# An attention and Hyena kernel: one list scheduler orders all engines, and keys, queries and x are turned by DMA

## The chip, the cores and the metric

The kernel runs on one NeuronCore of a Trainium2 chip. The core's engines are TensorE (PE), VectorE (DVE), ScalarE (ACT), GpSimd (POOL) and SyncE (SP, which here only issues DMAs). Sixteen DMA engines carry the transfers of all queues. The metric is the device time of one execution in microseconds (us), less is better.

## The reference

There are 8 batches, 12 heads, 448 positions and 64 dimensions a head (768 in all). First attention with a softmax whose denominator has one more term, then a gated convolution over the 448 positions, done by a Fourier transform:

```python
def _attn_ref(q, k, v):
    scores = scale * np.matmul(q, k.transpose(0, 1, 3, 2))
    m = np.max(scores, axis=-1, keepdims=True)
    e = np.exp(scores - m)
    attn = e / (np.sum(e, axis=-1, keepdims=True) + np.exp(-m) + 1e-09)
    return np.matmul(attn, v).astype(np.float32)

def _moe_ref(x, w_proj, filter_fft, w_out):
    proj = x @ w_proj
    x1, x2, x3 = (proj[..., :D].copy(), proj[..., D:2 * D].copy(), proj[..., 2 * D:].copy())
    X2 = np.fft.rfft(x2, n=S, axis=1)
    H = np.fft.rfft(filter_fft, n=S, axis=0)[None, :, :]
    x2_conv = np.fft.irfft(X2 * H, n=S, axis=1)
    y = x1 * x2_conv * x3
    return (y @ w_out).astype(np.float32)
```

Inputs and outputs are float32; x is the output of attention with the heads side by side.

## The kernel before

Work goes by batch, and in attention by pair of heads (six pairs a batch). For a pair, `transposes` (L321) turns keys and queries on PE with a matmul against the identity (L327, L329); DVE copies them out of PSUM, the keys into `kz`, where each head's keys stand beside zeros (L337, L338), the queries into `qT` (L345; L341 for batch 0, whose rows come in another order). `scores` (L348) has four steps: step 0 with the rest rows of both heads (L357, ACT's exponential at L359), steps 1 to 3 with two matmuls of 448 columns and an exponential of 896 (L353, L355). `attn_out` (L362) multiplies with the values in two halves (L367, L372); DVE divides by the sum (L380 to L382) into `xb`. `back` (L389) turns `xb` on PE (L395) and DVE copies it into `xT` (L398). After three pairs `folds` (L400) adds and subtracts halves of `xT` into `xf`.

`dense` (L463) makes a list of items for a batch: gate projections G (L508), the projection P of the folded x (L473, evicted by ACT at L480 into x2), the spectrum Z (L492 to L501), the inverse transform V (L532 to L547) and the output projection (L558, L580): four row tiles of 112 positions with two column halves, eight groups of six matmuls a batch. ACT evicts them (L568, L587) and SP stores them. "Dense stage" below is the run of these items for one batch. It runs beside the attention of the next batch, so that a period holds one attention and one dense stage; that of the last batch runs alone.

The order on PE, DVE, ACT and POOL is the order in which the program emits the calls (`manual_schedule`, L620). The main loop emits the attention items in a fixed order and after each takes dense items off the list in proportion to the cost, `RATIO = 1.9` (L615, L664). SP is ordered by the framework.

Batch 0 is loaded by SP in long rows as float32 into a stage of three buffers (`staged_load`, L130; casts on DVE and POOL, L160 to L182; the shared rest rows of keys by L164). Batches 1 to 7 are loaded by POOL's queue, which casts to bf16 on the way (`attn_load`, L111: four DMAs for queries at L115, eight for keys at L122 and L123, one for values at L124, then two copies of the rest rows of values, L109). The weights and the filter also come over POOL's queue (L282, L311, L317). `tables` (L185) builds the tables of the Fourier transform on DVE and ACT before anything else on DVE, and `filter_spectrum` (L292) transforms the filter with 16 matmuls (L303, L306) behind batch 0's attention.

Of the kernel before, what the change touches and what calls it, by code (L numbers as in the profile page):

```python
# [18 lines left out]
D = H * DH  # L19
# [8 lines left out]
Q0 = [0, 128, 256, 320]  # L28

# [6 lines left out]
BLK_K = [FQ, FQ, SP, SP]  # L36


@with_exitstack
def kernel(  # L40
# [13 lines left out]
    MAGIC = 12582912.0  # L54

# [7 lines left out]
    qtp = ctx.enter_context(tc.tile_pool(name="qtp", bufs=2))  # L63
# [21 lines left out]
    kn = [const.tile([128, NHP, 4, 128], BF16, name=f"kn{i}") for i in range(2)]  # L85
    vn = [const.tile([128, NHP, 7, DH + 1], BF16, name=f"vn{i}") for i in range(2)]
    vr = [const.tile([128, NHP, 2, DH + 1], BF16, name=f"vr{i}") for i in range(2)]
    kz = [const.tile([128, 8, 128], BF16, name=f"kz{i}") for i in range(3)]

    def constants(i):  # L90
        nc.gpsimd.memset(kn[i][:, :, 0, :], 0.0)
        nc.gpsimd.memset(vr[i], 0.0)
        nc.gpsimd.memset(vn[i][:, :, :, DH : DH + 1], 1.0)
        for u in range(2):
            nc.gpsimd.memset(vr[i][64 * u : 64 * u + 64, :, u, DH : DH + 1], 1.0)


    def batch_tiles(b):
        A = {"b": b, "kn": kn[b % 2], "vn": vn[b % 2], "vr": vr[b % 2]}
        A["qf"] = ld.tile([SP, NST, H, DH], BF16, name="qf")  # L100
        A["xb"] = xbp.tile([128, NST, H, DH], BF16, name="xb")
        A["xT"] = xtp.tile([128, NDT, S + 2], BF16, name="xT")
        A["xf"] = fold.tile([128, 4, NDT, FQ + 1], BF16, name="xf", tag="xf")
        return A

    def rest(A):
        for u in range(2):
            c = slice(64 * u, 64 * u + 64)
            nc.gpsimd.tensor_copy(A["vr"][c, :, u, 0:DH], A["vn"][c, :, 3, 0:DH])  # L109

    def attn_load(b):  # L111
        A = batch_tiles(b)
        kr = k[b].rearrange("h s d -> (h s) d").rearrange("(g t p) d -> p g t d", t=7, p=128)
        for st in range(NST):
            nc.gpsimd.dma_start(  # L115
                A["qf"][:, st, :, :],
                q[b, :, st * SP : (st + 1) * SP, :].rearrange("h p d -> p h d"),
            )
        for u in range(2):
            c = slice(64 * u, 64 * u + 64)  # L120
            for t in range(3):
                nc.gpsimd.dma_start(A["kn"][:, :, 1 + t, c], kr[:, :, 4 * u + t, :])  # L122
            nc.gpsimd.dma_start(A["kn"][c, :, 0, c], kr[c, :, 3, :])  # L123
        nc.gpsimd.dma_start(  # L124
            A["vn"][:].rearrange("p g t d -> p (g t) d")[:, :, 0:DH],
            v[b].rearrange("h s d -> (h s) d").rearrange("(n p) d -> p n d", p=128),
        )
        return A

    def staged_load(b, sp, tp):  # L130


        A = batch_tiles(b)
        A["staged"] = True

        def rows(x, hp):
            o = x[b, 2 * hp].offset
            return bass.AP(x.tensor, o, [[3 * DH, 128], [512 * DH, 2], [1, 3 * DH]])

        def shared(x):  # L140
            o = x[b].offset + 384 * DH
            return bass.AP(x.tensor, o, [[DH, 128], [2 * S * DH, NHP], [1, DH]])

        for hp in range(NHP):
            for name, x in (("k", k), ("q", q), ("v", v)):
                if name == "q":
                    t = A["sq", hp] = sp.tile([SP, 2, NST, DH], F32, name="sq")
                    nc.sync.dma_start(
                        t[:].rearrange("p u j d -> p u (j d)"),
                        q[b, 2 * hp : 2 * hp + 2].rearrange("u (p j) d -> p u (j d)", j=NST),  # L150
                    )
                    continue
                t = A[f"s{name}", hp] = sp.tile([128, 2, 3, DH], F32, name=f"s{name}")
                nc.sync.dma_start(t[:].rearrange("p u j d -> p u (j d)"), rows(x, hp))
                if hp == 0:
                    R = A[f"s{name}r"] = tp.tile([128, NHP, DH], F32, name=f"s{name}r")
                    nc.sync.dma_start(R, shared(x))
        return A

    def cast_shared(A, name, eng):  # L160
        for u in range(2):
            c = slice(64 * u, 64 * u + 64)
            if name == "k":
                eng.tensor_copy(A["kn"][c, :, 0, c], A["skr"][c])  # L164
            else:
                eng.tensor_copy(A["vr"][c, :, u, 0:DH], A["svr"][c])

    def cast_k(A, hp, eng):
        eng.tensor_copy(
            A["kn"][:, hp, 1:4, :].rearrange("p j (u d) -> p u j d", u=2), A["sk", hp]  # L170
        )

    def cast_q(A, hp, eng):
        dst = A["qf"][:, :, 2 * hp : 2 * hp + 2, :].rearrange("p j u d -> p u j d")
        if eng is nc.scalar:
            eng.copy(dst, A["sq", hp])
        else:
            eng.tensor_copy(dst, A["sq", hp])

    def cast_v(A, hp, eng):  # L180
        for u in range(2):
            eng.tensor_copy(A["vn"][:, hp, 4 * u : 4 * u + 3, 0:DH], A["sv", hp][:, u])  # L182


    def tables(tp):  # L185
        ci = tp.tile([128, HALF], I32, name="ci")
        nc.gpsimd.iota(ci[:], pattern=[[1, HALF]], base=0, channel_multiplier=0)
        pi = tp.tile([128, 1], I32, name="pi")
        nc.gpsimd.iota(pi[:], pattern=[[0, 1]], base=0, channel_multiplier=1)
        col = tp.tile([128, HALF], F32, name="col")  # L190
        nc.vector.tensor_copy(col, ci)
        row = tp.tile([128, 1], F32, name="row")
        nc.vector.tensor_copy(row, pi)
        col2 = tp.tile([128, 2, FQ], F32, name="col2")
        row2 = tp.tile([128, 2], F32, name="row2")
        for odd in range(2):
            nc.vector.tensor_scalar(
                col2[:, odd, :], col[:, 0:FQ], 2.0, float(odd), op0=ALU.mult, op1=ALU.add
            )
            nc.vector.tensor_scalar(  # L200
                row2[:, odd : odd + 1], row, 2.0, float(odd), op0=ALU.mult, op1=ALU.add
            )
# [8 lines left out]
        back = tp.tile([128, 1], F32, name="back")  # L211
        nc.vector.tensor_scalar(back, row, -1.0, float(SP), op0=ALU.mult, op1=ALU.add)
        inv = tp.tile([128, 1], F32, name="inv")
        nc.vector.tensor_scalar(inv, half, 2.0 / S, None, op0=ALU.mult)

        NF = 4 * FQ
        NB = 4 * HALF

        def sines(ph, n, tag):
            rd = hyp.tile([128, 2 * NF], F32, name="rd", tag="x2")  # L220
            nc.vector.tensor_scalar(rd[:, :n], ph, 1.0 / S, MAGIC, op0=ALU.mult, op1=ALU.add)
            nc.vector.tensor_scalar(rd[:, :n], rd[:, :n], -MAGIC, None, op0=ALU.add)
            nc.vector.scalar_tensor_tensor(
                ph, rd[:, :n], -float(S), ph, op0=ALU.mult, op1=ALU.add
            )
            sn = hyp.tile([128, 2 * NF], F32, name="sn", tag=tag)
            nc.scalar.activation(sn[:, :n], ph, AF.Sin, scale=float(2.0 * np.pi / S) * SHRINK)
            return sn

        pf = fold.tile([128, 2 * NF], F32, name="pf", tag="xf")  # L230
        pb = hyp.tile([128, NB], F32, name="pb", tag="yT")
        for pg in range(4):
            odd = int(BLK_ODD[pg])
            off = float(SP) if BLK_COS[pg] else 0.0
            nc.vector.tensor_scalar(
                pf[:, pg * FQ : (pg + 1) * FQ],
                col2[:, odd, :],
                row[:, 0:1],
                off,
                op0=ALU.mult,  # L240
                op1=ALU.add,
            )
            nc.vector.tensor_scalar(
                pf[:, NF + pg * FQ : NF + (pg + 1) * FQ],
                col2[:, odd, :],
                back[:, 0:1],
                off + (float(HALF) if pg in (1, 2) else 0.0),
                op0=ALU.mult,
                op1=ALU.add,
            )  # L250
            nc.vector.tensor_scalar(
                pb[:, pg * HALF : (pg + 1) * HALF],
                col,
                row2[:, odd : odd + 1],
                off,
                op0=ALU.mult,
                op1=ALU.add,
            )
        sf = sines(pf, 2 * NF, "yh")
        nc.vector.tensor_scalar(  # L260
            ft[:].rearrange("p a b -> p (a b)"), sf[:FQ, 0:NF], half[:FQ, 0:1], None, op0=ALU.mult
        )
        nc.vector.tensor_scalar(
            fr[:].rearrange("p a b -> p (a b)"),
            sf[:FQ, NF : 2 * NF],
            half[:FQ, 0:1],
            None,
            op0=ALU.mult,
        )
        sb = sines(pb, NB, "g")  # L270
        nc.vector.tensor_scalar(
# [148 lines left out]
    def attention():  # L420
# [4 lines left out]
        for p in range(len(pairs) + 1):  # L425
# [32 lines left out]
            for part in range(3):  # L458
                fd(part)
# [241 lines left out]
```

## Time and profile before

| | us |
|---|---|
| median of 3 runs | 472.2 (471.85 to 473.31) |
| the profiled execution | 474.68 |
| its span, first to last instruction | 472.9 |
| granted TensorE clock, mean | 0.988 |

The profile is of one execution. Its page gives busy time by engine, strips of 40 equal slices of the span with the busy share in tenths, and the costliest groups of instructions. In a row of groups stand: line, engine, operation, output tile, arrow, input tiles, shapes and count; behind the first bar busy us and mean ns of one; behind the second the idle us of the engine just before them and what ended it. In rows by order of time the first two numbers are start and duration. A matmul's duration contains its way through the array, which overlaps the next one, so its cost in a stream is the distance between starts.

### The profile page before, as it was taken

What the parts mean: (1) busy time and instruction counts of PE and PEld (TensorE: products, weight loads), DVE (VectorE), ACT (ScalarE), POOL (GpSimd) and SP (SyncE); (2) the same over time, 40 slices, a digit from 0 to 9 for tenths busy, and PEclk for the clock granted to TensorE, in tenths of its full rate; (3) what the DMA queues carried; (4) which work ended last, traced back from release to release, by engine and by line L of the source; (5) the groups of instructions that cost most, each with busy time, mean ns of one, the idle gap of its engine ahead of it and who ended that gap; (6) DMA issues with size and microseconds to landing.
All of it is one profiled execution on the core that took longest, in us unless ns stands there. A gap on an engine that the chain in (4) does not pass through costs nothing.

```text
span 472.9 us, 9624 instructions
## 1 busy us (share of the span) xinstructions
PE 426.3 (90%) x3872; PEld 298.9 (63%) x3872; DVE 307.3 (65%) x892; ACT 288.2 (61%) x493; POOL 109.4 (23%) x146
## 2 busy tenths in 40 slices
PE   0276889999999999999999999999999999999995
PEld 0144457577766777577766777577766777567664
DVE  7778555785569665774579575874578565873450
ACT  1364557666675667566675657657676668563543
POOL 5816391061202610071103510081000000000000
PEclk9998889999999999999999999999999999999999
DMA  7999999099901993097902991096900110003003
GB/s 208 181 231 176 146 161 62 1 73 134 89 1 11 138 129 19 1 88 120 89 1 20 144 129 5 1 101 126 69 1 1 60 60 0 2 2 119 0 1 116
DMA packets 128492, 35.62 MB, mean 75 GB/s; under 512 B 116925, under 2 KB 124864, under 8 KB 128448
## 3 DMA queue, kind: packets, MB, share of 16 engines
q0 software_dynamic: 118080, 19.87, 55.8%
q1 hardware_dynamic: 10368, 15.14, 10.9%
q8 instruction: 30, 0.49, 0.4%
q14 instruction: 14, 0.11, 0.1%
HBM read 43.86 MB, written 11.01 MB: 116 GB/s over the span
## 4 chain that ended last, share of the span: by engine, by line
PE 67%; DVE 14%; ACT 7%; DMA 7%; POOL 3%; issue 1%; SPq 1%; ACTq 0%; DVEq 0%; POOLq 0%
PE pps L508 18%; PE pps L473 10%; PE ops L580 10%; PE sc L353 9%; PE op L372 5%; DMA wproj_bf<-in_moe_w_proj_dram 4%; PE ops L558 3%; ACT xs L493 3%; PE cps L532 2%; PE xsp L492 2%; DVE t L496 2%; PE xps L395 2%; DVE g L519 2%; PE op L367 2%; DVE t L497 2%; ACT e L355 2%
## 5 line engine op out<-in xcount | busy, mean ns | idle before, releaser
L355 ACT ACTIVATE e<-sc 128x896 bf16<-128x896 f32 x144 | 132.6, 922 | 46.7 <-PE sc L353 46.7
L508 PE MATMUL pps<-xT,wproj_bf 128*128 128x448 bf16 x576 | 124.3, 352 | 0.5 <-ACT x L517 0.3
L508 PEld LDWEIGHTS <-wproj_bf 128*128 128x128 bf16 x576 | 53.5, 97 | 44.4 <-issue 3.0
L353 PE MATMUL sc<-qT,kz 128*128 128x448 bf16 x288 | 81.0, 364 | 0.5 <-ACT e L355 0.4
L473 PE MATMUL pps<-wproj_bf,xf 128*113 128x384 bf16 x384 | 72.2, 326 | 0.5 <-ACT x L480 0.5
L372 PE MATMUL op<-vn,e 128*128 128x65 bf16 x1152 | 58.1, 195 | 0.0
L473 PEld LDWEIGHTS <-xf 128*113 128x113 bf16 x384 | 48.9, 132 | 13.1 <-issue 0.9
L372 PEld LDWEIGHTS <-e 128*128 128x128 bf16 x1152 | 51.4, 98 | 6.8 <-issue 0.7
L580 PE MATMUL ops<-wout_bf,yT 128*112 128x384 bf16 x288 | 53.8, 327 | 0.5 <-ACT osb L568 0.5
L115 POOL DMA_DIRECT2D qf<-in_q_dram x28 | 26.2, 943 | 120.8 <-PE tps L329 84.1
L380 DVE TENSOR_SCALAR rec<-op 128x4 f32<-128x4 f32 x96 | 15.1, 158 | 56.9 <-PE op L372 56.7
L480 ACT CAST x<-pps 113x384 bf16<-113x384 f32 x64 | 30.8, 481 | 34.1 <-PE pps L473 33.8
L517 ACT CAST x<-pps 128x448 bf16<-128x448 f32 x48 | 25.5, 532 | 28.9 <-PE pps L508 26.5
L367 PE MATMUL op<-vr,er 128*128 128x130 bf16 x192 | 42.5, 221 | 0.5
L382 DVE TENSOR_TENSOR xb<-op,rec 128x256 bf16<-128x256 f32 x96 | 40.7, 424 | 3.3
L580 PEld LDWEIGHTS <-yT 128*112 128x112 bf16 x288 | 35.8, 130 | 10.1 <-issue 0.6
L327 PE MATMUL tps<-ident_bf,kn 128*128 128x128 bf16 x192 | 19.5, 224 | 22.1 <-DVE kn L164 18.9
L496 DVE TENSOR_TENSOR t<-xs,hrs 113x768 bf16<-113x768 bf16 (+1 forms) x32 | 17.8, 556 | 32.6 <-ACT xs L493 32.6
L587 ACT COPY osb<-ops 112x384 f32<-112x384 f32 x48 | 23.0, 480 | 23.9 <-PE ops L580 21.3
L353 PEld LDWEIGHTS <-kz 128*128 128x128 bf16 x288 | 27.3, 100 | 15.7 <-issue 3.1
L539 ACT CAST cw<-cps 128x448 bf16<-128x448 f32 x48 | 25.8, 539 | 18.3 <-PE cps L532 18.3
L398 DVE COPY xT<-xps 128x448 bf16<-128x448 bf16 x48 | 18.7, 389 | 26.5 <-PE xps L395 26.5
(97 smaller groups left out, 634.9 us busy)
## 6 DMA issues: line engine op xcount, KB each, us to landing
out_dram<-osb SPq DMA_DIRECT2D x32, 336.0 KB, 2.7
qf<-in_q_dram POOLq DMA_DIRECT2D x28, 168.0 KB, 5.4
vn<-in_v_dram POOLq DMA_DIRECT2D x7, 672.0 KB, 10.1
kn<-in_k_dram POOLq DMA_DIRECT2D x42, 96.0 KB, 4.7
wproj_bf<-in_moe_w_proj_dram POOLq DMA_DIRECT2D x3, 1152.0 KB, 14.0
sq<-in_q_dram SPq DMA_DIRECT2D x6, 224.0 KB, 6.5
sk<-in_k_dram SPq DMA_DIRECT2D x6, 192.0 KB, 6.4
sv<-in_v_dram SPq DMA_DIRECT2D x6, 192.0 KB, 4.6
```

Of the source, the lines that this page charges most:

```text
L115: nc.gpsimd.dma_start(A["qf"][:, st, :, :], q[b, :, st * SP : (st + 1) * SP, :].rearrange("h p d -> p h d"),)
L353: nc.tensor.matmul(sc[:, u, 0:S], P["z"][:, (4 - t, 4 + t)[u], :], P["qT"])
L355: nc.scalar.activation(e, sc[:, :, 0:S], AF.Exp, scale=SCALE)
L367: nc.tensor.matmul(op[:, i, :, :], e[0][:, qs], A["vr"][:, hp, :, :], start=True, stop=False)
L372: nc.tensor.matmul(op[:, i, u, :], e[1 + t][:, u, qs], A["vn"][:, hp, 4 * u + t, :], start=False, stop=(u == 1 and t == 2),)
L382: nc.vector.tensor_tensor(A["xb"][:, 2 * hf : 2 * hf + 2, 2 * hp : 2 * hp + 2, :], op[:, :, :, 0:DH], rec[:].unsqueeze(3).to_broadcast([12 ...
L473: nc.tensor.matmul(pps[:FQ, :DCH], xf[:, pg, kt, 0:FQ], wproj_bf[:, kt, D + ch * DCH : D + (ch + 1) * DCH], start=(kt == 0), stop=(kt == N ...
L480: nc.scalar.copy(T["x2"][:, pg, ch * DCH : (ch + 1) * DCH], pps[:FQ, :DCH])
L496: nc.vector.tensor_tensor(t1[:K], xs[:K], hrs[:K, par, :, cs], op=ALU.mult)
L508: nc.tensor.matmul(p[:, :S], wproj_bf[:, kt, 2 * part * D + dt * 128 : 2 * part * D + (dt + 1) * 128], xT[:, kt, 0:S], start=(kt == 0), st ...
L539: nc.scalar.copy(cw[:, dt % 2, :, :], cps[:, 0:S].rearrange("p (a n) -> p a n", a=2))
L580: nc.tensor.matmul(ops_[:SP, :DCH], yT[:, dt, st * SP : (st + 1) * SP], wout_bf[:, dt, ch * DCH : (ch + 1) * DCH], start=(dt == 0), stop=( ...
```

## The change

1. Every engine's instructions, SP's included, become tasks of a class `Plan`: engine, planned cost, wanted time, what it needs and makes, which buffers it takes and gives back. `run` plays the tasks in planned time, on each engine the first ready one by wanted time among 160, and emits them in that order. DMAs have a planned transfer time.
2. Keys and queries of batches 2 to 7 are loaded by POOL's queue as before into one buffer `nat`, and turned from there by DMAs of SP into `kT` and `qT`, a batch at a time. `nat` is also the stage of batches 0 and 1; its zero block for the keys is written behind the last cast of batch 1.
3. Batches 0 and 1 (`NSTAGED = 2`) come in long rows over SP and are turned on PE. The queries' copy out of PSUM moves from DVE to ACT.
4. The zeros move from the keys to the queries: POOL copies each head's half of `qT` into a zeroed `qz`, and the keys are used as they are. Step 0 uses `qT` itself.
5. x of the first five pairs is turned by two DMAs of SP a pair in batches 1 to 7; the sixth pair, and batch 0, by PE. `xb` has another layout for it.
6. The output projection uses row tiles of 128: three a batch, and one tile for the last 64 rows of two batches together, so 14 groups for two batches in place of 16.
7. P's second column half is evicted by DVE in place of ACT. The tables are smaller: one sine table, from which the others are made by PE, ACT and DVE. The filter's spectrum carries the factor 2/S.

The core of the diff:

```diff
+class Plan:
+    WINDOW = 160
+    LAT = {"PE": 0.2, "ACT": 0.12, "DVE": 0.12, "POOL": 0.15, "SP": 0.0}
...
+    def add(self, eng, cost, want, emit, need=(), make=(), take=(), give=(), dma=0.0, after=0.0):
+        self.tasks.append((want, len(self.tasks), eng, cost, emit, need, make, take, give, dma, after))
...
+            for e in queue:
+                if free[e] > now + 1e-9:
+                    continue
+                for i, t in enumerate(queue[e][: self.WINDOW]):
+                    if ready(t):
+                        break
...
+                if dma:
+                    other = rings["SP" if e == "POOL" else "POOL"]
+                    begin = max(rings[e], end)
+                    rings[e] = begin + dma * (1.6 if other > begin else 1.0)
+                    end = rings[e] + 1.8
...
+    NSTAGED = 2
...
+    kT = [const.tile([128, NHP, 4, 128], BF16, name=f"kT{i}") for i in range(2)]
+    qT = [const.tile([128, NHP, S], BF16, name=f"qT{i}") for i in range(2)]
+    qz = [const.tile([128, 2, S], BF16, name=f"qz{i}") for i in range(3)]
...
+    nat = const.tile([128, max(KNAT + NST * D, 6 * SLOT)], BF16, name="nat")
...
+    ATT0, SLOT0, PERIOD = 8.0, 3.6, 46.5
+    BASE = ATT0 + 6 * SLOT0
+    def tau(i, frac=0.0):
+        i += frac
+        return ATT0 + SLOT0 * i if i < NHP else BASE + (i - NHP) * PERIOD / NHP
...
+                    add("DVE", 0.25, want + 6.0, lambda c=c: nc.vector.tensor_copy(ks[c, :, c], rests[c, 0]),
+                        need=[("rk", b), "zero ks"] + ([("T", NHP * b - 1)] if b else []), make=[("crk", b)])
...
+    def loaded(b):
+        want = tau(i0) - 40.0
+        room = ["zero kn" if b == NSTAGED else ("turn", b - 1)]
...
+            need=room + [("V", i0 - NHP - 1, 1)], make=[("vn", b)], dma=6.0)
...
+        def q_turn(st):
+            nc.sync.dma_start(
+                qT[b % 2][:, :, st * SP : (st + 1) * SP], qn[:, st], transpose=True
+            )
+        def k_turn(gs):
+            nc.sync.dma_start(
+                kT[b % 2][:, gs].rearrange("p g t c -> p (g t) c"),
+                kn[:, gs].rearrange("p g t c -> p (g t c)"),
+                transpose=True,
+            )
+        last = ("S", i0 - NHP - 1, 3)
...
+        def spread(u):
+            c = slice(64 * u, 64 * u + 64)
+            nc.gpsimd.tensor_copy(z[c, u, :], qT[b % 2][c, hp, :])
+        for u in range(2):
+            add("POOL", 0.6, tau(i) - 4.0 + 0.1 * u, lambda u=u: spread(u),
+                need=[("qT", i), ("zero", "q")] + ([("S", i - 3, 3)] if i >= 3 else []),
+                make=[("qz", i)])
...
+            if t:
+                for u in range(2):
+                    nc.tensor.matmul(sc[:, u, 0:S], kT[b % 2][:, hp, t, :], z[:, u, :])
...
+        def x_dma():
+            x, xb = xT(), W["xb", b]
+            nc.sync.dma_start(
+                x[:, hp, 0:384].rearrange("p (t n) -> p t n", t=3), xb[:, hp, 0:3, :].rearrange("p t c -> p (t c)"), transpose=True
+            )
+            nc.sync.dma_start(x[:, hp, 384:S], xb[64:128, hp, 3, :], transpose=True)
...
+        if b and hp < NHP - 1:
+            add("SP", 0.8, w, x_dma, need=[("xb", i)] + old, make=[("X", i), ("xT", b, hp // 3)], dma=0.5)
         else:
+            add("PE", 0.23, w, x_pe, need=[("xb", i)], make=[("X", i)], take=[("hy", ("X", i))])
...
+            y = W["yT", b][:, :, st * 128 : (st + 1) * 128] if st < 3 else W["yR", b // 2]
...
+        for st in range(3 if b % 2 == 0 and b + 1 < n_batches else 4):
+            for ch in range(2):
+                O(st, ch)
...
-        tc.manual_schedule(engines={E.PE, E.Pool, E.DVE, E.Activation}),
+        tc.manual_schedule(engines={E.PE, E.Pool, E.DVE, E.Activation, E.SP}),
...
+        add("DVE", 0.5, BASE, lambda: nc.vector.memset(kn[:, :, 0, :], 0.0),
+            need=[("c" + x, g) for x in "kqv" for g in range(6, 12)], make=["zero kn"])
+        for part, w, g in ((1, 14.0, 2), (0, 20.0, 4), (2, 26.0, 5)):
+            add("POOL", 1.3, w, lambda part=part: wproj_load(part), need=[("cv", g)], make=[("w", part)],
+                dma=5.1, after=w)
+        add("POOL", 3.0, 34.0, filter_load, need=[("cv", 6)], make=["filt"], take=[("yT", "F")], dma=3.5,
+            after=34.0)
+        add("POOL", 1.3, 44.0, wout_load, need=[("cv", 7)], make=["wout"], dma=5.1, after=44.0)
...
+        plan.run()
```

More of the change, by code (lines that the diff above doesn't have):

```diff
@@ L463, in dense @@
-    def dense(A):
-        b, xT, xf = A["b"], A["xT"], A["xf"]
-        T = {}
+        for g in range(2):
+            w = ready - (0.4 if g else PERIOD / 4 if b else 4.0)
+            for n in range(2):
+                add("DVE", 0.62 - 0.1 * n, w, lambda g=g, n=n: first(g, n),
+                    need=[("xT", b, g)] + ([("fold", b, g, 0)] if n else []), make=[("fold", b, g, n)],
+                    take=[("uw"[n], (b, g))])
+                for pg in (2 * n, 2 * n + 1):
+                    add("DVE", 0.34, w, lambda g=g, pg=pg: second(g, pg), need=[("fold", b, g, n)],
+                        make=[("xf", b, pg)], take=[("xf", b)], give=[("uw"[n], (b, g))])
@@ L503, in gate @@
+            for n in range(2):
+                tk = (f"t{n}", (b, par, ch))
+                add("DVE", 0.57, w + 1.0, lambda n=n: product(par, ch, n),
+                    need=[("xs", b, par, ch), ("hrs", par)], make=[("t", b, par, ch, n)],
+                    take=[tk], give=[xs])
+                add("DVE", 0.37, w + 1.5, lambda n=n: total(par, ch, n), need=[("t", b, par, ch, n)],
+                    make=[("yh", b)], take=[("yh", b)], give=[tk])
         def gate(dt, part):
-            if "g" not in T:
-                T["g"] = hyp.tile([128, NDT, S], BF16, name="g", tag="g")
```

1046 lines of the change are left out of this document (608 added, 438 removed).

## The prediction

> **What bounds the kernel now.** I read the page's busy rows and its strips first, then the windows of single stages, then the order of time inside one stage, and only then the waits.
>
> ```profile
> span 472.9 us, 9624 instructions
> PE 426.3 (90%) x3872; PEld 298.9 (63%) x3872; DVE 307.3 (65%) x892; ACT 288.2 (61%) x493; POOL 109.4 (23%) x146
> PE   0276889999999999999999999999999999999995
> PEclk9998889999999999999999999999999999999999
> 162.60:215.20 52.60, 51.61 (x484) 36.65 (x483) 35.33 (x105) 34.72 (x61) 13.03 (x15) 1.00 0.72 67
> 30.00:35.00 5.00, 3.41 (x50) 2.24 (x48) 4.37 (x13) 3.19 (x4) 0.95 (x1) 1.00 1.14 233
> ```
>
> The strip of PE has two parts: six slices (70 us) in which it fills up, and 33 slices at nine tenths. The window 162.6 to 215.2 (busy us and counts of PE, PEld, DVE, ACT, POOL, then clock, DMA share, GB/s) is one batch of the second part: PE is busy 51.61 of 52.60 us, at full clock, while DVE has 35.33 and ACT 34.72. There only PE work counts, and 1.0 us of holes. In 30 to 35 us it is otherwise: PE 3.41 of 5, DVE 4.37 of 5. The start is bound by DVE, and by what it waits for:
>
> ```profile
> 18.89 0.58 PE L327 MATMUL tps<-ident_bf,kn 128*128 128x128 bf16 x4 [18.89 <-DVE kn L164]
> 31.77 0.35 PE L357 MATMUL sc<-qT,kz 128*128 128x448 bf16 x1
> 36.67 0.35 PE L357 MATMUL sc<-qT,kz 128*128 128x448 bf16 x1
> 47.18 4.15 DMA kn<-in_k_dram
> 65.76 1.30 PE L508 MATMUL pps<-xT,wproj_bf 128*128 128x448 bf16 x6
> 432.77 2.44 PE L508 MATMUL pps<-xT,wproj_bf 128*128 128x448 bf16 x12
> ```
>
> (Columns of the order of time: start, us, engine, line, tile; the fourth row is of the chain of waits.) The first matmul comes at 18.9, behind DVE's tables and casts. A head pair of batch 0 takes 36.67 - 31.77 = 4.9 us. At 47 to 51 the chain stands on batch 1's keys. The first dense stage begins at 65.8, the last at 432.8: seven periods of (432.77 - 65.76) / 7 = 52.43 us, and 472.9 - 432.77 = 40.1 us behind the last.
>
> **The steady stage: what leaves PE.**
>
> ```profile
> 202.71 0.39 PE L327 MATMUL tps<-ident_bf,kn 128*128 128x128 bf16 x4
> 202.94 0.36 PE L329 MATMUL tps<-ident_bf,qf 112*128 112x112 bf16 x4
> 203.13 0.55 PE L532 MATMUL cps<-bt,yh 113*128 113x224 bf16 x4
> 207.44 0.39 PE L395 MATMUL xps<-ident_bf,xb 128*128 128x128 bf16 x4
> 207.67 0.35 PE L357 MATMUL sc<-qT,kz 128*128 128x448 bf16 x1
> 217.71 1.14 PE L580 MATMUL ops<-wout_bf,yT 128*112 128x384 bf16 x6
> 218.69 0.22 PE L367 MATMUL op<-vr,er 128*128 128x130 bf16 x1
> ```
>
> Since matmuls overlap, an item costs the distance to the next start. Turning keys and queries of a pair: 203.13 - 202.71 = 0.42. Turning x of a pair: 0.23. One output group: 0.98. Batches 2 to 7 lose six key and query turns each, 2.52 us; batches 1 to 7 lose five of six x turns, 1.15 us; two batches need 14 output groups in place of 16, 0.98 us a batch. Scores keep two matmuls of 448 columns, since the zeros only move from keys to queries. A period with the old holes is 52.43 - 2.52 - 1.15 - 0.98 = 47.78. The 1.0 us of holes may go, as the list scheduler puts ready work there, or grow, as its costs are fixed numbers. I take them as gone, **46.8 us**, and keep 45.8 (the matmul records overlap, so there are more holes than shown) and 48.8 for the range.
>
> Next in line would be DVE and ACT. DVE also loses the copies of those turns:
>
> ```profile
> L337 DVE COPY kz<-tps 64x512 bf16<-64x512 bf16 x48 | 19.7, 411 | 10.7 <-PE tps L329 10.7
> L345 DVE COPY qT<-tps 128x448 bf16<-128x448 bf16 x42 | 16.4, 391 | 0.6
> L398 DVE COPY xT<-xps 128x448 bf16<-128x448 bf16 x48 | 18.7, 389 | 26.5 <-PE xps L395 26.5
> L480 ACT CAST x<-pps 113x384 bf16<-113x384 f32 x64 | 30.8, 481 | 34.1 <-PE pps L473 33.8
> ```
>
> With the twin of L337 at the same price, 6 x (0.41 + 0.41 + 0.39) + 5 x 0.39 = 9.2 us a batch go; half the x2 evictions come to DVE from ACT, 4 x 0.48 = 1.9. Both engines then stand near 28 and 33 of 46.8: hidden, and with that cover gone DVE would still have 18 us to spare.
>
> **What is added there.** POOL writes the zero-padded queries, two copies of 64x448 a pair; SP issues 16 turning DMAs a batch.
>
> ```profile
> L109 POOL COPY vr<-vn 64x384 bf16<-64x384 bf16 x14 | 7.4, 531 | 57.1 <-DMA vn<-in_v_dram 56.8
> 170.53 2.04 POOL L124 DMA_DIRECT2D vn<-in_v_dram  x1 [9.55 <-issue]
> DMA  7544170699999000000000000000000079999999
> q0 software_dynamic: 16442, 2.08, 63.2%
> q1 hardware_dynamic: 512, 1.38, 8.5%
> ```
>
> (The last three: the DMA part of 162.6 to 215.2, with 40 slices of 1.315 us; queue, packets, MB, packet time.) A padding copy is some 0.53 x 448 / 384 = 0.62 us, 7.4 a batch on top of 13.0: POOL stays under half. But scores now wait for POOL, and the issue of the values stood 9.55 us for nothing that the profile shows; whatever is queued behind it on POOL stands too. A pair's queries may be padded once the third pair before it has its scores, some two pairs or 15 us ahead, so I cost this at nothing, and at 9.55 us a batch in a rival.
>
> No turning DMA is in this trace. Its bytes a batch: queries 4 x 112 x 768 x 2 = 0.69 MB, keys 2 x 128 x 1536 x 2 = 0.79, x 5 x (128 x 384 + 64 x 128) x 2 = 0.57, in all 2.05 MB. The nearest rows are the output stores on the same SP queue, 1.38 MB in 8.5% of 52.6 us, or 309 GB/s: 6.6 us a batch; and the loads of POOL's queue, 2.08 MB in 63.2%, or 63 GB/s: 33 us. The strip has 20 of 40 slices empty, so 26 us a batch are in use. At 6.6 us all of it fits into 46.8; at 33 it would not. I take the first, as it is the same queue and as large in its pieces, and keep the second as a rival. Keys and queries are needed a batch later, so their latency hides; x of the last pair still goes by PE. The waits of the turning DMAs hold SP, and behind them stand stores with two buffers: hidden as long as SP runs a few us late at most. The Trainium skill (DMA: Bandwidth & Descriptors, Latency and other measured facts) gives 261 GB/s for a turning DMA with a broken-up middle dimension; by that the estimate is 7.8 us in place of 6.6, and the sum is the same.
>
> **The start.** Batch 1 now comes in rows over SP as batch 0 does, so the wait at 47 us goes. DVE builds a quarter of the phase table (4 of 12 pieces, one rounding of 452 columns for two of 900).
>
> ```profile
> L223 DVE SCALAR_TENSOR_TENSOR pf<-rd,pf 128x904 f32<-128x904 f32 x1 | 1.3, 1287 | 0.0
> L164 DVE CAST kn<-skr 64x384 bf16<-64x384 f32 x2 | 1.6, 812 | 0.0
> L382 DVE TENSOR_TENSOR xb<-op,rec 128x256 bf16<-128x256 f32 x96 | 40.7, 424 | 3.3
> L341 DVE COPY qT<-tps 128x448 bf16<-128x448 bf16 x6 | 6.9, 1152 | 0.1
> L355 ACT ACTIVATE e<-sc 128x896 bf16<-128x896 f32 x144 | 132.6, 922 | 46.7 <-PE sc L353 46.7
> L359 ACT ACTIVATE er<-sc 128x448 bf16<-128x448 f32 x48 | 26.3, 547 | 8.4 <-PE sc L357 8.4
> ```
>
> DVE ahead of the first turn: some 5 us of tables and zeros, 1.6 for the two shared-key casts of 0.81, 0.8 for the other casts, so about 9 us in place of 18.9. Three more (as from 18.89 to the first score at 22) and a padding copy of 1 give the first exponential at 13. A pair then costs ACT 3 x 0.92 + 0.55 and the query copy, between 0.53 (a plain ACT eviction of 448) and 1.15 (L341, the same scattered write on DVE): 3.8 to 4.5; I take 4.1, nearer to ACT's own row. DVE has less, since L341 and a twin of L337 leave it. So 13 + 6 x 4.1 + 3 for the last output, turn and folds: the first dense stage begins at **40**, where 36 is the least (10, 3.8, 3) and 52 the most (4.9 a pair and 5 us of waiting for DMA again).
>
> **The sum, against the profiled execution.** 40 + 7 x 46.8 = 367.6. Batch 1 is still turned on PE: + 2.5. The filter's 16 matmuls now come behind the first dense start:
>
> ```profile
> 65.25 0.33 PE L303 MATMUL hps<-uw,ft 113*112 113x384 bf16 x1
> 65.41 0.33 PE L306 MATMUL hps<-uw,fr 113*112 113x384 bf16 x1
> ```
>
> 16 x 0.16 = + 2.6. Batch 2's loads need the memory of batch 1's last staged pieces (tile nat), near 62 us; with 20 us for keys and queries (151.0 to 170.5 in the steady stage) and the turn they come near 90. PE has batch 1's dense stage by then, but attention falls behind: between 0 and 14 us, I take + 4. Behind the last dense start 40.1, unchanged (batch 7 keeps eight output groups). Span: 367.6 + 2.5 + 2.6 + 4 + 40.1 = 416.8, against 472.9. The profiled execution took 474.68, 1.8 more than its span and 2.5 more than the median 472.2; with the same ends, 416.8 + 1.8 - 2.5 = 416, said as **416 us**.
>
> **The rivals.**
>
> *POOL and the fixed order stall PE.* All engines run in an order set by planned costs. The trace speaks for slips: the shared-key cast is planned at 0.25 where its row says 0.81, and nothing is planned for the 9.55 us stand. If padding copies stand behind it without their lead, six batches cost up to 57 us. Half of that gives 416 + 29 = 445. Against it: the values' load waits for the outputs of two batches before, so it will often come long after the keys, when its queue is empty.
>
> *The start doesn't shorten*, since the weights and two staged batches share the DMA engines (busy in every slice up to 75 us): the first dense stage stays near 65, and the time is 416 + 25 = 441.
>
> *DMA becomes the bound: slower.* At the second price, 26 + 33 = 59 us of DMA a batch, six batches of 59 in place of 46.8 make 416 + 73 = 489. It decides from (472 - 416) / 6 = 9.3 us over the period, 56 us a batch, which is 30 us of turning, 68 GB/s. Against it: the one queue that SP has runs at 309 GB/s today. The Trainium skill (Advanced Engine Details and Errata, DGE: Hardware vs Software) calls turning on the hardware queues less efficient and gives no figure; no run here shows it.
>
> *The holes vanish altogether and the start is at its least*: 7 x 1 + 4 + 4 less, 401.
>
> That the change doesn't take the turns off PE is hardly a case: those calls are gone for 36 of 48 pairs.
>
> **How the numbers follow.** Forecast (406 to 432): 0.58. Stalls (432 to 462): 0.20. No shorter start: 0.08. Better than 406: 0.07. DMA-bound: 0.07. The range must leave out no more than 0.2: from 402 (most of the better case) to 448, which holds the start rival and two thirds of the stalls. About 0.3%, or 1.4 us, is what a measurement of this kernel can tell; every case but the last is faster by more, so faster 0.92, within 0.01, slower 0.07.
>
> **What would show it.** Right: a period near 46.8 between dense starts, PE near 46 of it, the first L508-like group near 40 us, turning DMAs landing within some us. Wrong: PE idle before scores with POOL or a DMA as releaser (stalls), the DMA strip at nine throughout (DMA-bound), the first dense start past 50 us. A lower granted clock from holes in PE would cost beyond the holes themselves.

## The result, and the profile after

The changed kernel takes **445.7 us** (median of 4, 443.2 to 448.6) against 472.8 (median of 4, 471.9 to 474.7): 0.942 of the time, 95% interval 0.936 to 0.949. It gains 27 us where 56 were forecast, and lies inside the range. The times of kernels here and below are medians of executions whose mean granted clock was 0.95 or more; one execution of e1 below, the profiled one, took 592 us at 0.66 and is left out, so that e1 has a time but no trace to read. The first rows are of the page after (busy rows and strips), then come the stages between dense starts (length, then busy us and count of PE, PEld, DVE, ACT and POOL, clock, DMA share, GB/s; the DMA share of this view adds up the times of packets and can exceed 1).

```profile
span 443.6 us, 9006 instructions
PE 397.9 (90%) x3401; PEld 262.2 (59%) x3401; DVE 274.8 (62%) x788; ACT 277.7 (63%) x465; POOL 159.4 (36%) x237
PE   1785999897999859998999969999999999999895
PEclk9998899999999979999999988999999999999998
```

```profile
48.72:105.96 57.24, 52.27 (x468) 35.07 (x467) 36.96 (x105) 38.97 (x67) 30.43 (x42) 1.00 1.17 141
105.96:155.66 49.70, 47.73 (x415) 31.55 (x414) 34.88 (x98) 33.22 (x56) 32.12 (x40) 1.00 1.59 145
155.66:210.11 54.45, 48.10 (x405) 31.44 (x402) 29.80 (x83) 31.13 (x54) 19.35 (x25) 0.94 0.88 100
210.11:259.57 49.46, 47.60 (x416) 31.68 (x415) 32.90 (x96) 33.27 (x57) 22.35 (x29) 1.00 1.16 118
259.57:312.39 52.82, 48.20 (x403) 31.57 (x402) 29.96 (x83) 31.09 (x54) 19.00 (x25) 0.94 0.97 103
312.39:360.04 47.65, 47.23 (x415) 31.58 (x414) 32.75 (x93) 33.59 (x58) 9.22 (x14) 1.00 0.73 81
360.04:402.93 42.89, 42.80 (x380) 28.89 (x378) 27.16 (x82) 28.18 (x49) 2.45 (x4) 1.00 0.16 42
```

PE's busy time fell by 28.4 us (426.3 to 397.9), but its idle time is the same, 45.7 us where it was 46.6. So what left PE was gained, and the idle time in sum did not shrink. The span is 26.8 us longer than the forecast 416.8:

| stage | forecast | measured | off |
|---|---|---|---|
| first dense start | 40.0 | 48.72 | +8.7 |
| period 1 (46.8 + 2.5 + 2.6) | 51.9 | 57.24 | +5.3 |
| period 2 (46.8 + 4) | 50.8 | 49.70 | -1.1 |
| periods 3 and 5 | 93.6 | 107.27 | +13.7 |
| periods 4, 6 and 7 | 140.4 | 140.00 | -0.4 |
| behind the last dense start | 40.1 | 40.67 | +0.6 |

Periods 3 and 5 stand out: the clock is 0.94 there, and the strip of PE, behind its start, has a 5 and a 6. The timeline of SP's queue at the first of these places (start, duration, line), and after it the rows of ACT and PE:

```profile
144.15 6.00 SPq L378 DMA_TRANSPOSE qT<-nat  x4
150.24 0.53 SPq L909 DMA_DIRECT2D out_dram<-osb  x1
151.07 2.27 SPq L383 DMA_TRANSPOSE kT<-nat  x1
153.45 1.33 SPq L909 DMA_DIRECT2D out_dram<-osb  x1
154.88 4.16 SPq L383 DMA_TRANSPOSE kT<-nat  x1
159.13 0.56 SPq L909 DMA_DIRECT2D out_dram<-osb  x1
```

```profile
148.23 0.86 ACT L902 COPY osb<-ops 128x384 f32<-128x384 f32 x2
153.25 0.86 ACT L902 COPY osb<-ops 128x384 f32<-128x384 f32 x2 [0.35 <-DMA out_dram<-osb]
162.54 0.86 ACT L902 COPY osb<-ops 128x384 f32<-128x384 f32 x2 [7.17 <-DMA out_dram<-osb]
163.07 1.28 PE L795 MATMUL pps<-xT,wproj_bf 128*128 128x448 bf16 x3 [5.24 <-ACT osb L902]
```

The first store stands behind query turns until 150.24. ACT had copied the rows of the second by 149.1. Its issue stands on SP behind a key turn until 153.45, and the chain of waits gives its landing (start, us):

```profile
153.45 8.99 DMA out_dram<-osb
```

Only at 162.44 does the second of two buffers come free; ACT, whose order is fixed, has stood 7.17 us for it, PE 5.24, and PE's next work runs slow (three windows of the changed kernel):

```profile
155.00:160.00 5.00, 2.83 (x28) 1.66 (x26) 1.36 (x5) 0.37 (x1) 0.27 (x1) 1.00 1.90 142
160.00:165.00 5.00, 1.93 (x6) 0.80 (x6) 0.00 (x0) 2.12 (x4) 0.00 (x0) 0.63 1.67 197
165.00:170.00 5.00, 5.00 (x22) 3.34 (x21) 1.18 (x2) 1.94 (x3) 2.00 (x4) 0.68 1.32 236
```

The granted clock is 0.63 and 0.68 in the last two. The same happens near 260 us: a store leaves at 255.78, between two key turns, lands 8.84 us later, and PE stands 3.51 us.

### The profile page after: what moved, and what is told of

It reads as the page before. It is cut to its first block, busy times and chain, and to the rows that moved or that the text cites. A ratio compares the mean times of both kernels' runs of the same rounds, so it can differ in the third digit from the quotient of the medians.

```text
span 443.6 us, 9006 instructions
## 1 busy us (share of the span) xinstructions
PE 397.9 (90%) x3401; PEld 262.2 (59%) x3401; DVE 274.8 (62%) x788; ACT 277.7 (63%) x465; POOL 159.4 (36%) x237
## 4 chain that ended last, share of the span: by engine, by line
PE 68%; DMA 12%; DVE 10%; ACT 4%; POOL 2%; issue 2%; SPq 0%; DVEq 0%; ACTq 0%; POOLq 0%
PE pps L795 19%; PE pps L722 15%; PE ops L890 10%; PE sc L571 9%; PE op L603 6%; DMA out_dram<-osb 5%; DMA xT<-xb 5%; DMA nat<-in_v_dram 3%; PE cps L829 3%; ACT e L579 2%; PE xsp L749 2%; PE op L598 2%; DVE g L810 2%; DVE yT L864 2%; DVE cv L849 1%
## 5 line engine op out<-in xcount | busy, mean ns | idle before, releaser
L560 POOL COPY qz<-qT 64x448 bf16<-64x448 bf16 x96 | 62.1, 647 | 166.8 <-PE sc L571 120.6
L571 PE MATMUL sc<-qz,kT 128*128 128x448 bf16 x288 | 79.1, 364 | 4.9 <-POOL qz L560 3.8
L890 PE MATMUL ops<-wout_bf,yT 128*128 128x384 bf16 x288 | 52.2, 326 | 2.2 <-DVE yT L864 2.1
L902 ACT COPY osb<-ops 128x384 f32<-128x384 f32 x56 | 25.3, 483 | 33.7 <-DMA out_dram<-osb 16.7
L810 DVE TENSOR_TENSOR g<-x,pps 128x448 bf16<-128x448 bf16 x48 | 29.7, 618 | 26.9 <-PE pps L795 19.6
L890 PEld LDWEIGHTS <-yT 128*128 128x128 bf16 x288 | 27.0, 98 | 22.7 <-DVE yT L864 4.9
L763 DVE TENSOR_TENSOR t<-xs,hrs 113x768 bf16<-113x768 bf16 (+1 forms) x64 | 37.7, 617 | 3.9 <-ACT xs L757 3.9
L571 PEld LDWEIGHTS <-kT 128*128 128x128 bf16 x288 | 24.6, 100 | 18.2 <-issue 7.8
L736 ACT CAST x<-pps 113x384 bf16<-113x384 f32 x32 | 15.5, 486 | 26.7 <-PE pps L722 26.7
L734 DVE CAST x<-pps 113x384 bf16<-113x384 f32 x32 | 17.8, 555 | 23.0 <-PE pps L722 23.0
## 6 DMA issues: line engine op xcount, KB each, us to landing
wproj_bf<-in_moe_w_proj_dram POOLq DMA_DIRECT2D x3, 1152.0 KB, 13.4
```

Of the source, the lines that this page charges most:

```text
L560: nc.gpsimd.tensor_copy(z[c, u, :], qT[b % 2][c, hp, :])
L571: nc.tensor.matmul(sc[:, u, 0:S], kT[b % 2][:, hp, t, :], z[:, u, :])
L763: nc.vector.tensor_tensor(t[:K], L["xs", par, ch][:K], h, op=ALU.mult)
L810: nc.vector.tensor_tensor(g[:, dt, :], L["x1", dt], p[:, :S], op=ALU.mult)
L890: nc.tensor.matmul(ops[:n, :DCH], y[:, dt, 0:n], wout_bf[:, dt, ch * DCH : (ch + 1) * DCH], start=(dt == 0), stop=(dt == NDT - 1),)
```

## The experiments

Theory A: the stores stand behind turning DMAs on SP, and that makes the two stops. Its rival: the turns' and the loads' bytes on the DMA engines hold the stores, wherever they are issued. Theory C is about the start: POOL, whose order is fixed too, stands for a value load while scores wait for the padding copy behind it. Each ratio is against runs of the kernel before that were taken beside it on the same chip, so the ratios are safer to compare than the times.

| kernel | us | ratio, 95% interval |
|---|---|---|
| e1 third store buffer | 437.2 | 0.921 (0.916 to 0.926) |
| e2 stores from ACT | 433.5 | 0.917 (0.913 to 0.921) |
| e9 both | 434.1 | 0.915 (0.911 to 0.919) |
| e3 keys, queries by PE | 441.9 | 0.933 (0.930 to 0.936) |
| e4 x by PE | 436.3 | 0.921 (0.918 to 0.925) |
| e12 e2 and x by PE | 436.1 | 0.920 (0.917 to 0.923) |
| e8 values after the turns | 446.3 | 0.942 (0.938 to 0.946) |
| e13 keys in six turns | 448.2 | 0.948 (0.942 to 0.953) |
| e5 value casts later | 452.4 | 0.955 (0.948 to 0.961) |
| e7 one staged batch | 457.7 | 0.967 (0.963 to 0.971) |
| e10 earlier loads | 449.8 | 0.951 (0.946 to 0.956) |
| e11 e2, e5 and e10 | 438.6 | 0.925 (0.921 to 0.929) |
| e14 e11 and x by PE | 436.6 | 0.923 (0.920 to 0.926) |
| e15 e11, half of x by PE | 437.2 | 0.923 (0.919 to 0.927) |

**e1: a third buffer.**

```diff
-otp = ctx.enter_context(tc.tile_pool(name="otp", bufs=2))
+otp = ctx.enter_context(tc.tile_pool(name="otp", bufs=3))
```

> One more output row buffer on the chip, the planned order unchanged. Theory A (the two PE stops at 158 to 163 and 260 to 265 us come from stores that land 9 us late while ACT has only two row buffers): ACT's wait for stores (16.7 us, 8 times) falls below 6, the two stops shrink to under 2 us each, and with the slow-clock stretches behind them the time falls by 8 to 14 us, to 432 to 438. Theory B (the DMA engines are full there, and PE would stop for the next transfer anyway): less than 3 us, 443 to 446.

437.2 us, in Theory A's range. The wait for a store's buffer is worth some 8 us, whatever makes the store late. Only the time speaks here; that the two stops shrank isn't shown.

**e2: the same stores from ACT's queue.**

```diff
-nc.sync.dma_start(out[b, st * 128 : (st + 1) * 128, :], osb)
+nc.scalar.dma_start(out[b, st * 128 : (st + 1) * 128, :], osb)
```

(And the packed rows of L912 likewise.)

> Output stores are issued by ACT instead of SP, at the same places of the planned order. If the stores are late because they stand behind key turns on SP's queue: the longest landing of a store falls from 10.0 to under 5 us, ACT's wait for stores from 16.7 to under 5, time 430 to 438. If they are late because all queues share engines that are full of the values' small packets and the turns: the longest landing stays over 8 us and the time within 3 us of 445.

433.5 us. The timeline of ACT's issues in this kernel, and its windows of periods 3 and 5:

```profile
149.11 0.34 ACTq L909 DMA_DIRECT2D out_dram<-osb  x1
150.30 0.34 ACTq L909 DMA_DIRECT2D out_dram<-osb  x1
154.49 0.34 ACTq L909 DMA_DIRECT2D out_dram<-osb  x1
```

```profile
156.47:204.78 48.31, 45.62 (x404) 30.51 (x402) 29.96 (x84) 31.20 (x54) 19.06 (x25) 1.00 1.22 115
253.57:300.19 46.62, 45.50 (x403) 30.50 (x402) 29.68 (x83) 30.69 (x52) 19.04 (x25) 1.00 1.21 117
```

The second store leaves 3.15 us earlier, ahead of the key turns. Periods 3 and 5 lose 6.14 and 6.20 us, together the whole difference of the spans (443.6 to 431.3), and the clock is back at 1.00. PE's work in the two shrinks by 2.5 and 2.7 us with the same matmuls, but for one: that much was the low clock. Neither branch of the expectation is right in full: landings did not get shorter (median 3.6 us after 3.5, the longest 13.0 after 10.0), yet the time fell as the queue theory says. The store that had stopped PE did land sooner: leaving at 150.30 in place of 153.45 it took 4.5 us in place of 9.0. The one behind it, issued at 154.49, took the 13.0, and PE did not wait for it. What counts is when a store is issued, and whether anything waits for the one that lands late. The Trainium skill (DMA: Bandwidth & Descriptors, Rules for kernel authors) says that spreading DMAs over issuing engines doesn't help bandwidth and only saves the sequencer's issue time. The medians of the landings agree. The order on the issuing queue is worth 12 us of the span here.

**e9: both cures.**

> Edit: output stores issued from ACT's queue and three buffers instead of two for the stored rows; the order of all engines as the scheduler then makes it. Theory A (what was lost against the forecast in the steady stage is mostly the wait of the evictions for stores that stand behind turning DMAs on SP; either cure takes it away): the two cures overlap, so little is added to ACT's stores alone: 430 to 434. Rival (the landing times of stores still cost, since they stayed as long with ACT's issue): a third buffer hides them too, 425 to 429.

434.1 us, no more than e2. With the stores off SP the third buffer has nothing to hide, as Theory A has it.

**e3 and e4: less on SP.** e3 turns keys and queries of batches 2 to 7 by PE, x stays with the DMAs; e4 turns x by PE, keys and queries stay.

```diff
 # e4
-if b and hp < NHP - 1:
+if False:
```

> Edit: keys and queries of batches 2 to 7 turned by PE as before the change, with their copies on DVE; x stays with the DMAs. PE gains 36 turns of 0.42 us, 15.1 us. Theory A (the key and query turns on SP are what the stores stand behind): the two stops of PE near 160 and 260 us go, some 11 us with the lower clock behind them, and the time is 446 to 452, within a few us of the changed kernel's 445.7. Rival (the stops have another cause, and the turns save what PE's rows say): 457 to 463.

> Edit: x of all pairs turned by PE, as before the change; keys and queries stay with the DMAs. PE gains 35 turns of 0.23 us, 8 us, and SP loses 70 turning DMAs. Theory A (the long key turns block the stores, the short x turns hardly): the stops stay, 451 to 456. Rival (SP as a whole is too full, and each DMA taken from it gives stores and keys back): 438 to 446.

e3 ran 441.9 us: PE does 13 us more work than in e2 (406.6 after 393.2), the stops are gone, and the time is better than the changed kernel's. Theory A stands, though the time lies 4 us under its range. e4 ran 436.3, and there my Theory A, which laid the stops on the key turns alone, missed: the rival is right. Each x turn holds SP too. (e4 also takes the bytes of these turns off the DMA engines; that the place on the queue matters is shown by e2 and e13, which leave the bytes as they are.) The rows of x, one line and the other, in the changed kernel:

```profile
L642 SPq DMA_TRANSPOSE xT<-xb x35: 1191/1195/3649, 57.8 to 394.4; - x35
L645 SPq DMA_TRANSPOSE xT<-xb x35: 1205/1218/2017, 59.1 to 395.6; - x35
```

(ns, least, median and most.) Five pairs a batch are 5 x (1.195 + 1.218) = 12.1 us of SP; with the four query turns (6.00, above) and the two key turns (2.27 + 4.16) it is 24.5 us a batch.

**e12: e2, and x by PE.**

> Edit: stores from ACT's queue, and x of all pairs turned by PE. With ACT's stores alone PE's stops are gone, so PE's 8 us of x turns should show: 438 to 441. Rival (turning x by DMA costs in waits and in late folds what it saves on PE): 432 to 436.

436.1 us: the rival, at its upper edge. PE works 7 us more than in e2 (400.3 after 393.2) and idles 5 us less, and the intervals of the two ratios overlap. Turning x by DMA is worth at most a few us on this kernel even with the stores elsewhere, and as the change has it, it costs 9 (e4 against the changed kernel).

**e8: the load of the values behind the key turns.**

```diff
-need=room + [("V", i0 - NHP - 1, 1)], make=[("vn", b)], dma=6.0)
+need=room + [("V", i0 - NHP - 1, 1), ("kT", i0), ("kT", i0 + 3)], make=[("vn", b)], dma=6.0)
```

> The values' load of a batch waits in the plan until its keys have been turned, so that its 5376 small packets do not run beside the turns and stores. If the values' load is what makes turns and stores late: the keys' turn lands in under 5 us instead of a median of 9.9, stores in under 5 us at most, time 430 to 438. If a key turn is slow by itself: its landing stays near 9 us and the time within 3 us of 445.

446.3 us. Issue to landing of the key turns, in the changed kernel and then in this one:

```profile
kT<-nat SPq DMA_TRANSPOSE x12, 9.9
```

```profile
kT<-nat SPq DMA_TRANSPOSE x12, 4.2
```

So what makes a key turn land late is the load of the values that runs beside it. It has a part in the late stores too: PE's waits for them are 3.7 us in this kernel, where they were 8.7. But the time is the same: in the new order PE stands 4.27 us at 112.5 for a turn of x which was issued at 104.00 and landed 8.49 later. A quicker turn is worth nothing while one queue's fixed order decides who waits.

**e13: keys in six turns.**

```diff
-for h in range(2):
-    gs = slice(3 * h, 3 * h + 3)
+for h in range(NHP):
+    gs = slice(h, h + 1)
...
```

> Edit: the keys of a batch turned by six DMAs of one pair each instead of two of three pairs; everything else, the stores on SP among it, as in the changed kernel. The scheduler can now put stores between short turns: in the first stop the second store comes ahead of all key turns, in the others one short turn stands ahead of it instead of one long one. Theory (a store issued behind a long key turn is late and lands late): the two stops of PE shrink from 5 us each to under 1 us, the granted clock stays at 1.00 in both stages, and the time is 433 to 438. Rival (the turns' bytes on the engines, not their order on SP, hold the stores): the stops stay and the time is 443 to 448.

448.2 us, the rival's time, and yet not its mechanism. The windows of the stages with stops, and SP and PE earlier in this kernel:

```profile
171.72:219.44 47.72, 45.64 (x404) 30.52 (x402) 28.76 (x83) 31.37 (x54) 20.76 (x28) 1.00 1.16 110
268.38:315.03 46.65, 45.53 (x404) 30.52 (x403) 29.11 (x83) 31.23 (x54) 19.77 (x26) 1.00 1.15 113
```

```profile
96.19 8.68 SPq L383 DMA_TRANSPOSE kT<-nat  x6
104.98 1.05 SPq L909 DMA_DIRECT2D out_dram<-osb  x2
106.12 2.54 SPq L642 DMA_TRANSPOSE xT<-xb  x1
108.72 1.23 SPq L645 DMA_TRANSPOSE xT<-xb  x1
```

```profile
115.62 2.80 PE L795 MATMUL pps<-xT,wproj_bf 128*128 128x448 bf16 x7 [8.94 <-DMA xT<-xb]
```

Both stops for stores are gone, as Theory A expected: periods 3 and 5 at 47.7 and 46.7, clock 1.00. But batch 2's six turns now hold SP for 8.68 us where two held it for 3.29, a turn of x stands behind them, and PE stands 8.94 us for that. Near 149 us it stands 5.85 more, for a result of DVE that waits for another turn of x; that turn was issued at 143.41, behind key turns which had held SP for 5.26 us. Period 2 is 66 us in place of 49.7. The same queue, another victim.

**e5, e7 and e10: the start.** In the changed kernel POOL waits for a value load that takes 13.21 us, the padding copy stands behind it, and PE behind that (the chain, then POOL and PE in order of time):

```profile
28.02 13.21 DMA nat<-in_v_dram
```

```profile
41.72 0.83 POOL L285 CAST vn<-nat 128x192 bf16<-128x192 f32 x2 [3.61 <-DMA nat<-in_v_dram]
42.49 1.17 POOL L560 COPY qz<-qT 64x448 bf16<-64x448 bf16 x2
43.10 1.90 PE L571 MATMUL sc<-qz,kT 128*128 128x448 bf16 x4 [2.13 <-POOL qz L560]
```

```diff
 # e5: a value cast behind the padding copy of the pair before
-add("POOL", 0.9, tau(g) + 1.0, cast, need=[("sv", g)], make=[("cv", g), ("v", g)])
+add("POOL", 0.9, tau(g) + 1.0, cast, need=[("sv", g)] + ([("qz", g - 1)] if g else []), make=[("cv", g), ("v", g)])
 # e7
-NSTAGED = 2
+NSTAGED = 1
...
 # e10, with the casts no longer needed ahead of either load
-for part, w, g in ((1, 14.0, 2), (0, 20.0, 4), (2, 26.0, 5)):
+for part, w, g in ((1, 9.0, 2), (0, 15.0, 4), (2, 21.0, 5)):
...
-add("POOL", 3.0, 34.0, filter_load, need=[("cv", 6)], make=["filt"], take=[("yT", "F")], dma=3.5,
-    after=34.0)
+add("POOL", 3.0, 28.0, filter_load, make=["filt"], take=[("yT", "F")], dma=3.5,
+    after=28.0)
```

> On POOL a staged pair's value cast stands behind the query padding of the pair before it, instead of up to two pairs ahead. Theory C (the first dense stage begins at 48.7 instead of 40 us because padding copies stand on POOL behind casts that wait for late value loads): PE's waits for padding (3.8 us) and ACT's waits for scores near 36 to 44 us go, the first dense stage begins at 42 to 45, and the time falls by 3 to 6 us, to 439 to 443. Rival (the start is held by the loads of batch 1 themselves, which DMA brings at its full rate): dense start within 1 us of 48.7, time 444 to 447.

> Edit: one staged batch instead of two; batch 1 is loaded and turned as batches 2 to 7 are. If the second staged batch is what makes the start shorter: second and first dense stage late, 455 to 470. If it does nothing for the start or its loads only take DMA time from batch 0: 440 to 448, with the first dense start a few us earlier than 48.7.

> Edit: the loads of the projection weights and of the filter wait for no cast of values in the plan, and are wanted 5 to 6 us earlier; POOL issues them a few places earlier in its order. Theory (the start is held by DMA: weights and staged pieces share full engines from 25 us on, while they stand nearly empty near 20 us): the first weights take the empty stretch, batch 1's values land sooner, the first dense stage begins at 43 to 46 instead of 48.7 and the time falls by 2 to 4 us, 441 to 444. Rival (the start is set by the order on POOL and by batch 1's pair put ahead of it on PE): the first dense stage stays at 47 to 50 and the time at 444 to 448.

e5 moves the first dense start to 44.76: that wait on POOL is worth 4 us of the 8.7 that the start is late. Half of the 4 is clock: up to the first dense start PE has 311 matmuls in the changed kernel and 312 in e5, which take 30.0 and 27.8 us at granted clocks of 0.93 and 1.00. But the second dense start stays at 106.50, and at 452.4 us nothing is gained. e7 ran 457.7, with the first dense start at 53.08 and the second at 117.77: two staged batches do shorten the start. e10 left the start at 48.68, so the place of the weights in POOL's order isn't what holds it; at 449.8 the time is above both branches, with PE's stops for stores at 11.1 us.

**e11, e14 and e15: everything together.** e11 is e2 with e5 and e10; e14 adds x of all pairs by PE, e15 only that of the last three of a batch.

```diff
 # e15
-if b and hp < NHP - 1:
+if b and hp < NHP - 3:
```

> Edit: three edits at once: stores from ACT's queue, the casts of values behind the padding copy of the pair before on POOL, and the earlier loads of weights and filter. If the start's loss and the store stops are separate and the late filter load was what took the first one's gain back: 433.5 less some 4 us, 427 to 430, with the first dense stage at 42 to 45 and the second at 101 to 103. If the second dense stage stays at 105 to 107 whatever the first does: 433 to 435.

> Edit: the three edits of the kernel before it (stores from ACT's queue, casts of values later on POOL, loads of weights and filter earlier), and x of all pairs turned by PE, so that SP's queue holds only the turns of keys and queries behind the start. Theory (that kernel's earlier start was lost again because turns of x stand behind the key turns on SP, which held SP for 10 us near 100 us): the first dense stage begins at 43 to 46, no period has a stop over 2 us, and the time is 436.1 less the 3 to 4 us of the start, 431 to 434. Rival (an earlier dense stage only waits elsewhere, for attention of batch 1): 435 to 438.

> Edit: as the kernel before it in this call, but x of the first three pairs of a batch still turned by DMA, and only that of the last three by PE (14 more turns of 0.23 us on PE than with the change, 3.2 us). Theory: the turns that dense stages wait for are those of the late pairs; with them on PE the stop near 105 us goes, and 3 us more of PE are paid: 429 to 433, with the first dense stage at 43 to 46. Rival (any turn of x behind a key turn delays the folds): a stop of over 3 us stays and the time is 434 to 440.

e11's first and second dense starts come at 45.15 and 103.02, as wanted, but 438.6 us is outside both branches. SP and the chain in it:

```profile
96.41 10.21 SPq L383 DMA_TRANSPOSE kT<-nat  x2
```

```profile
137.35 5.17 DMA xT<-xb
```

The key turns hold SP for 10.2 us, and period 2 takes 62 us. e14 takes x off SP, and no such stop is left; its dense starts are 45.22, 99.50 and 154.68, where e12, without the earlier start, has 47.41, 105.02 and 154.11. The third is no earlier, and the times are alike (436.6 and 436.1). So the rival holds: an earlier first dense stage is given back before the third. In the two periods between, PE idles 6.2 us in e14 and 4.4 in e12, and as many matmuls but one take 1.0 us longer. Why, the runs don't settle. e15 keeps a stop of 3.6 us (for a result of DVE) and ran 437.2, in the rival's range. e2 remains the best, level with e9.

## Why the prediction missed

**The step that failed** is "hidden as long as SP runs a few us late at most", and the term under it, 6.6 us of turning a batch. That term is bytes over a rate, of the DMA engines. The resource that the turns take is SP, and there they cost 24.5 us of a 47 us period, near the other end that I named (33) and set aside as a rival about the engines. An engine-bound period did not come: periods 3 and 5, which have the stops, show a DMA share of 0.88 and 0.97, less than periods 2 and 4 (1.59 and 1.16), which have none. What came is a queue in a fixed order. SP was no more than a few us late, and that was not hidden: a store 3.2 us late, a landing of 9.0, two buffers, and 12.3 of the 26.8 us, in periods 3 and 5, which e2 gives back (6.14 and 6.20; its other stages differ by up to 0.7 us each and cancel). The traffic has a part in it, since the share is 1.90 and 1.67 in the ten us around the first stop: the store that left 3.15 us earlier in e2 landed in 4.5, and e8, with the values' load moved away, has less than half of the wait. e3, e4 and e13 remove the stops in three more ways, with the stores still on SP; e13, e8 and e11 show the same queue making another wait.

**"The 1.0 us of holes may go ... I take them as gone"** was wrong. Two windows from first to last dense start, of the kernel before and of e2:

```profile
65.76:432.77 367.01, 359.08 (x3351) 254.93 (x3350) 245.58 (x729) 240.38 (x417) 72.11 (x83) 1.00 0.61 58
48.79:391.00 342.21, 329.09 (x2892) 219.77 (x2891) 225.59 (x637) 230.02 (x392) 135.37 (x178) 1.00 1.08 110
```

The kernel before had 367.0 - 359.1 = 7.9 us of PE idle there; the changed one has 20.3, and e2, without the stops for stores, still 342.2 - 329.1 = 13.1. Five of these are in period 1, where PE's 52.27 us of work are what I summed (51.9). In the changed kernel they are many waits of at most 1.0 us each, for results of DVE and ACT; what would remove them was not tried.

**The start**: 4 us are POOL's wait (e5). The sum itself slipped: 13 + 6 x 4.1 + 3 is 40.6, said as 40, and 4.9 us a pair with 5 us of waiting gives 50.4, said as 52. The first exponential came at 13.7, where 13 was said, and batch 0's pairs follow each other at 4.2 us, near the 4.1, although ACT's query copy took 1.15 us (L324), the upper end of its bounds. "6 x 4.1 + 3" left out what the order puts ahead of the dense stage. Two rows of PE, the scores of batch 1's first pair and the turn of its second:

```profile
39.62 0.35 PE L573 MATMUL sc<-qT,kT 128*128 128x448 bf16 x1 [0.27 <-ACT e L579]
45.69 0.30 PE L308 MATMUL tps<-ident_bf,ks 128*128 128x128 bf16 x1
```

Both come before 48.72. That this makes the rest of the 8.7 was not tried.

**Right**: the PE terms. The forecast has 336.7 us between first and last dense start, 332.7 of work and 4 of waiting; e2 has 329.1 of work there. Turning on PE cost nearly what its rows said (13.4 us more in e3, 15.1 by the rows; 7.1 in e12, 8 by the rows). The end of 40.1 held within 0.6. Period 2 held within 1.1, but not by its terms: its work is 47.7 us for 46.8, its idle time 2.0 for 4.

**The rivals.** The time is that of *POOL and the fixed order stall PE*, 445, and that is luck: the number was half of six stands of 9.55 us at the issue of the values, which are gone. A fixed order did stall PE, but in the steady stage it was SP's; POOL's padding copies held PE only ahead of the first dense start, for 3.8 us. That the time lies in the range is owed to this rival and the next one, for whose sake the range went up to 448. (It holds about half of the stalls, 432 to 448 of 432 to 462, and not two thirds.) *The start doesn't shorten* didn't come (65.8 to 48.7), nor did *DMA becomes the bound*.

## What to carry to other kernels

Work that moves from an engine to DMAs is paid twice: in bytes on the DMA engines, and in the time that each issue holds its queue. Add up the second by queue, with everything else that stands there, and ask of each late item who waits for it with how many buffers. A queue that issues long items wants no short ones with two buffers behind them; another issuer for these, or a third buffer, was worth more here than any change of the long ones. Taking the x turns off the queue was worth as much as the third buffer.

## What the runs showed of the hardware

A turn of 96 KB or less holds SP as long as the shortest key turn of 384 KB: 1.2 us for either part of an x turn (96 KB and 16 KB), and 1.27 at least for a key turn. The most was 5.1 us in the changed kernel and 10.9 in e2, in this view of its key turns (ns):

```profile
L383 SPq DMA_TRANSPOSE kT<-nat x12: 1273/2818/10933, 96.2 to 300.4; - x12
```

In the window of a stop of PE of 5 us and in the one after it the granted clock was 0.63 and 0.68. The matmuls of the two periods with stops (of 5.24 and 3.51 us) took 2.5 and 2.7 us longer than those of e2 without them: half of the first stop again, and more of the second.
